# Attention and a mixture of experts in one kernel: the experts' token lists built by comparisons and matmuls of ones instead of scatters

## The chip, the core and the metric

One core of a Trainium2 chip runs the whole kernel. Its engines are TensorE (PE, whose weight loads are shown as PEld), VectorE (DVE), ScalarE (ACT), GpSimd (POOL) and SyncE (SP). The metric is the time of one execution on the device in microseconds (us). The trace counts from the start of its span.

## The reference

Attention of 8 batches, 8 heads, 576 positions and 64 dimensions, then a mixture of 8 experts over the 4608 tokens. Each token goes to the one expert with the largest logit, so the experts' work depends on lists of tokens that exist only once attention is done.

```python
q_rot, k_rot = (rotate(q), rotate(k))
scores = scale * np.matmul(q_rot, k_rot.transpose(0, 1, 3, 2))
attn = np.exp(scores - np.max(scores, axis=-1, keepdims=True))
attn = attn / (np.sum(attn, axis=-1, keepdims=True) + 1e-09)
x = np.matmul(attn, v)  # then heads are put side by side: 4608 tokens x 512
logits = x @ w_gate
e_idx = np.argmax(logits, axis=1)
gate_w = softmax(logits)[np.arange(N), e_idx]
eom = 1.0 / (1.0 + np.exp(-(x @ w_output_gate)))
for e in range(E):
    mask = e_idx == e
    h = np.maximum(x[mask] @ w1[e], 0.0)
    out[mask] = gate_w[mask, None] * eom[mask, e, None] * (h @ w2[e])
```

## The kernel before

The order of all instructions is written out by hand.

**Attention** goes over 32 pairs of heads (4 pairs to a batch). A pair has 9 steps; a step is one tile of 128 queries by 576 keys. In each step PE makes the scores in one of two PSUM buffers (`scores`, tag `sc`, L432 and L439), DVE takes their maximum (`peak`, L445), ACT makes the exponentials (`exp`, L454), and one step later DVE transposes them in blocks (`turn`, L460). All the rest is hung on steps: `EVENTS` gives, for every piece of work of a pair, its step counted from the pair's first and its place in the step. So the values of a pair (`values`, L479) are multiplied in steps 2, 4, 6 and 8 of the next pair; `back` (L494), which turns the result and multiplies it with the gates' weights, and `divide` (L502 to L511) come in its step 1; POOL rotates and splits the queries and keys of later pairs (`mult` L388, `add` L392, `keylo` and `querylo` L372) in steps 5, 7, 8, 1, 3 and 5. SP loads `raw` (queries and keys of a pair, L377) and `v` (L383).

**Placing a batch.** `place` makes a list of small functions, one to a step, that begins 20 steps after the first step of the batch's last pair. They find each token's expert (`s0` to `s7`), its output weight (`s8` to `s12`), and write the batch's tokens, 513 numbers a row, to the DRAM tensor `xd` (`s13`, two stores from SP, L590 and L591). `s14` ranks the tokens: two matmuls of ones and of a triangle (L599, L600) into `rk`, a tile taken from the same two score buffers; DVE reads it (L602, L603). `s15` to `s17` make each token's place `pi` in a long list: one stretch of 4608 places for each expert. Then five indirect DMAs from POOL (`scatter`, L616) write the token numbers, 4 bytes each, to these places, each into a DRAM list of its own, `lst0` to `lst4`; SP filled them at the start with a large number (L166). In steps of a pair, `s13` falls on a step 6, `s14` on a step 0 and the scatters on steps 6, 7, 8, 0 and 1. POOL does the elementwise steps, except in the last batch, where DVE does.

**Tables.** A table says which rows (128 tokens of one expert) a run of slots works on. Table 0 (5 slots of two rows) is made in attention, table 1 (in two parts: 9 slots of two rows, 15 of one, numbered 2 and 1) in the first expert slots. `slots` computes the row numbers on DVE, fills five tiles `tk` on POOL (L701), gathers them with five indirect DMAs from the five lists (L706), takes their minimum (four DVE instructions, L713), turns it on PE (L717) and casts it to indices. `pieces` cuts this into functions, one to a step.

**Experts.** `fetch` gathers the tokens of the first two slots (`xg`, L832), in a buffer that `xb`, the tokens of a batch, also uses. Each slot has eight steps: four of the first matrix (L888, L898), four of the second (L926). Weights come from SP (`wr`, L845), ACT and DVE or POOL split them in two (L854, L856), POOL scatters the results to the output (L938). The last batch's placing and table 1 are a queue, `left`, from which each of the eight steps of a slot takes two functions; the last batch's five scatters share entries with table 1's first five functions.

Of the kernel before, what the change touches and what calls it, by code (L numbers as in the profile page):

```python
# [10 lines left out]
F32 = mybir.dt.float32  # L11
# [25 lines left out]


# [15 lines left out]
C_E8, C_MASK, C_TOK, C_EB, C_SL, C_TRI, C_ONE = range(7)  # L54
# [16 lines left out]
def const_table(nb):  # L71
# [41 lines left out]
def body(ctx, tc, nb, offs, qk, v, rope, cst, gates, w, out):  # L113
# [39 lines left out]
    zero, big = stage[:, nst:nst + 256], stage[:, nst + 256:nst + 256 + nl // P]  # L153
    nc.vector.memset(zero, 0.0)
    nc.vector.memset(big, BIG)
# [4 lines left out]
    def consts():  # L160
        nc.vector.tensor_copy(ii[:, :, 0:P], ident.unsqueeze(1).broadcast_to((P, NP, P)))
        nc.vector.tensor_copy(trib, sc(C_TRI))
        nc.vector.tensor_copy(oneb, sc(C_ONE))
        nc.vector.memset(cnt, 0.0)
        for l in lst:
            nc.sync.dma_start(out=l.rearrange("(p n) o -> p (n o)", p=P), in_=big)  # L166

    att = Attention(tc, nb, pools, cc, ident, ii, first, trib, oneb, cnt, zero, qk, v, xd, lst)
    n0 = slot_counts(nb)[0]
    moe = Moe(tc, nb, (px, px2, small), cc, ident, cnt, w, xd, lst, out)  # L170
# [47 lines left out]
class Attention:  # L218


    def __init__(self, tc, nb, pools, cc, ident, ii, first, trib, oneb, cnt, zero, qk, v, xd, lst):
# [33 lines left out]
        for n, pr in enumerate(self.pairs):  # L255
# [259 lines left out]
def place(tc, pools, b, NT, cc, trib, oneb, cnt, xbs, xd, lst):  # L515
# [71 lines left out]
    def s13():  # L587
# [4 lines left out]
        V.tensor_scalar(new("tok", [P, NCH]), cc(C_TOK), float(b * S), None, op0=ALU.add)  # L592
# [21 lines left out]
    def scatter(c):  # L614
        m = QR if c == 4 else P
        nc.gpsimd.indirect_dma_start(  # L616
            out=lst[c][:, :], out_offset=bass.IndirectOffsetOnAxis(ap=T["pi"][:m, c:c + 1], axis=0),
            in_=T["tok"][:m, c:c + 1], in_offset=None, bounds_check=E * list_rows(NT // S) - 1, oob_is_err=False)
# [16 lines left out]
class Moe:
# [40 lines left out]
    def slots(self, n, m, ends, delta, first, step, wait):  # L676
# [28 lines left out]
        for l, tk in zip(self.lst, tks):  # L705
# [343 lines left out]
```

## Time and profile before

| | us |
|---|---|
| median of 3 runs | 1230.01 |
| lowest, highest | 1220.46, 1232.24 |
| the profiled execution | 1221.57 |
| its span | 1219.8 |
| last exponentials of attention start | 681.4 |
| first matmul of the experts starts | 717.5 |

| engine | busy us | share of the span |
|---|---|---|
| PE | 1074.2 | 88% |
| DVE | 835.0 | 68% |
| ACT | 640.2 | 52% |
| POOL | 597.9 | 49% |

The page shows one execution. A row of the timeline has start, length, engine, line, operation, what it writes and reads, how many are merged, and in brackets how long the engine stood idle before it and what ended that. A row of groups has count, busy us, mean ns of one, and idle time before with what ended it; "issue" is a wait for nothing that the profile shows. A row of waits has total us, times and the longest. Rows of stretches have, for every engine, busy us and number of instructions, then the granted share of TensorE's clock, the busy share of the DMA engines and GB/s. PEclk is that clock in 40 slices, in tenths, 9 being 90% or more.

### The profile page before, as it was taken

How to read it: one execution, taken by the hardware profiler on the slowest of the kernel's cores; microseconds unless marked ns; L12 is line 12 of the kernel's file. 1: busy time of each engine (PE TensorE's matmuls, PEld its weight loads, DVE VectorE, ACT ScalarE, POOL GpSimd, SP SyncE). 2: the span in 40 equal slices, each digit the busy share in tenths (PEclk: the TensorE clock that was granted, in tenths of full speed). 3: DMA queues.
4: the chain of work that ended last, by engine and by line, in shares of the span. 5: the costliest groups of instructions: out<-in, count | busy, mean ns of one | idle time of the engine just before them, and what ended most of it. 6: DMA issues, size and time to landing. Idle time of an engine off the chain costs nothing.

```text
span 1219.8 us, 34628 instructions
## 1 busy us (share of the span) xinstructions
PE 1074.2 (88%) x14419; PEld 919.9 (75%) x14419; DVE 835.0 (68%) x1335; ACT 640.2 (52%) x1309; POOL 597.9 (49%) x535
## 2 busy tenths in 40 slices
PE   3999985999887888989857879989999999999998
PEld 2877764777766766777646578878988989889986
DVE  6788863876765766767747347655677786786784
ACT  3566642554543544545424245433576675686573
POOL 4676765566774675575554312332154253353242
PEclk9999987988987998878868869989999999999999
DMA  6544486484675675574724647956578788797791
GB/s 206 157 143 134 120 165 80 111 164 112 153 126 86 159 113 140 131 126 110 162 36 79 213 139 210 239 191 214 185 253 301 266 298 278 272 330 263 269 338 40
DMA packets 55713, 216.87 MB, mean 178 GB/s; under 512 B 10337, under 2 KB 11260, under 8 KB 47488
## 3 DMA queue, kind: packets, MB, share of 16 engines
q1 hardware_dynamic: 46432, 194.77, 59.0%
q0 software_dynamic: 8160, 19.03, 4.6%
q8 instruction: 115, 1.88, 0.7%
q10 hardware_dynamic: 960, 0.82, 0.2%
q14 instruction: 46, 0.38, 0.1%
HBM read 195.98 MB, written 20.70 MB: 178 GB/s over the span
## 4 chain that ended last, share of the span: by engine, by line
PE 65%; DVE 12%; issue 9%; DMA 5%; ACT 4%; another core or an unknown queue 2%; POOL 2%; SPq 0%; POOLq 0%; ACTq 0%; DVEq 0%
PE py L926 15%; PE acc L479 14%; PE sc L439 14%; PE ph L898 12%; PE ph L888 4%; DVE pt L460 3%; DVE m L445 3%; PE sc L432 3%; DMA wr<-in_w 2%; PE acc L494 2%; ACT pm L454 2%; DVE wl L856 1%; PE mtp L870 1%; DMA lst<-tok,pi 1%
## 5 line engine op out<-in xcount | busy, mean ns | idle before, releaser
L454 ACT ACTIVATE pm<-sc,m 128x576 f32<-128x576 f32 x288 | 213.2, 740 | 283.1 <-DVE m L445 281.3
L445 DVE TENSOR_REDUCE m<-sc 128x1 f32<-128x576 f32 x288 | 213.7, 742 | 171.2 <-PE sc L439 156.0
L856 DVE TENSOR_TENSOR wl<-wr,wh 128x1024 fp32r<-128x1024 f32 x183 | 252.2, 1389 | 68.3 <-ACT wh L854 66.3
L479 PE MATMUL acc<-pt,v 32*64 32x160 f32 (+1 forms) x9216 | 240.1, 322 | 58.1 <-issue 33.0
L439 PE MATMUL sc<-kh,q 64*128 64x288 f32 x1024 | 239.9, 345 | 54.3 <-ACT pm L454 39.5
L479 PEld LDWEIGHTS acc<-pt,v 32*64 32x64 f32 x9216 | 184.0, 145 | 97.3 <-issue 65.0
L439 PEld LDWEIGHTS sc<-kh,q 64*128 64x128 f32 x1024 | 164.1, 207 | 103.3 <-ACT pm L454 55.8
L460 DVE STREAM_TRANSPOSE pt<-pm 128x576 f32<-128x576 f32 x288 | 220.5, 766 | 12.5 <-ACT pm L454 11.6
L854 ACT CAST wh<-wr 128x1024 fp32r<-128x1024 f32 x208 | 213.1, 1051 | 4.5 <-DMA wr<-in_w 4.4
L926 PE MATMUL py<-wh,ht 128*128 128x512 f32 x640 | 213.8, 399 | 0.0
L898 PE MATMUL ph<-xt,wh 128*128 128x256 f32 x896 | 165.9, 288 | 4.1 <-ACT xb L511 4.1
L388 POOL TENSOR_TENSOR raw<-raw,rt 128x1152 f32<-128x1152 f32 x62 | 164.0, 2646 | 9.4 <-DMA raw<-in_qk 9.3
L898 PEld LDWEIGHTS ph<-xt,wh 128*128 128x128 f32 x896 | 142.9, 195 | 6.1 <-ACT xb L511 4.6
L926 PEld LDWEIGHTS py<-wh,ht 128*128 128x128 f32 x640 | 120.2, 188 | 24.0
L898 PE MATMUL ph<-xt,wl 128*128 128x256 f32 x448 | 128.2, 286 | 0.0
L926 PE MATMUL py<-wl,ht 128*128 128x512 f32 x320 | 125.1, 391 | 0.0
L439 PE MATMUL sc<-kl,q 64*128 64x288 f32 x512 | 118.0, 315 | 0.0
L856 POOL TENSOR_TENSOR wl<-wr,wh 128x1024 fp32r<-128x1024 f32 x25 | 61.1, 2445 | 109.4 <-ACT wh L854 95.5
L439 PEld LDWEIGHTS sc<-kl,q 64*128 64x128 f32 x512 | 92.3, 210 | 0.0
L392 POOL TENSOR_TENSOR raw<-raw 128x576 f32<-128x576 f32 x62 | 87.8, 1416 | 3.2
L372 POOL TENSOR_TENSOR kl<-raw,kh 128x576 fp32r<-128x576 f32 x31 | 44.0, 1418 | 92.2 <-ACT kh L364 92.1
L898 PEld LDWEIGHTS ph<-xt,wl 128*128 128x128 f32 x448 | 87.2, 195 | 0.0
(208 smaller groups left out, 1303.0 us busy)
## 6 DMA issues: line engine op xcount, KB each, us to landing
wr<-in_w SPq DMA_DIRECT2D x208, 512.0 KB
v<-in_v SPq DMA_DIRECT2D x128, 288.0 KB
raw<-in_qk SPq DMA_DIRECT2D x31, 1152.0 KB
xd<-xb SPq DMA_DIRECT2D x8, 1026.0 KB
raw<-in_qk SPq DMA_DIRECT2D x2, 576.0 KB
xd<-xb SPq DMA_DIRECT2D x8, 128.2 KB
lst<-stage SPq DMA_DIRECT2D x5, 144.0 KB
lst<-tok,pi POOLq DMA_INDIRECT x40
```

What stands on the lines that cost most here:

```text
L388: self.eng(eng).tensor_tensor(out=rv, in0=rv, in1=self.rt[:, 2 * t:2 * t + 2, x], op=ALU.mult)
L392: self.eng(eng).tensor_tensor(out=r[:, 2 * t, x], in0=r[:, 2 * t, x], in1=r[:, 2 * t + 1, x], op=ALU.add)
L439: nc.tensor.matmul(ps[:, a, :HS], self.q[r, w, c * P:c * P + P], mov[r, a * HS:a * HS + HS], start=(n == 0), stop=(n == 2))
L445: nc.vector.tensor_reduce(self.m[i], ps[:, :, :HS], axis=AX.XY, op=ALU.max, negate=True)
L454: nc.scalar.activation(pe.rearrange("p (a b) -> p a b", a=2), self.ps[i][:, :, :HS], AF.Exp, bias=self.m[i], scale=1.0, accum_out=self.z[: ...
L460: self.nc.vector.transpose(out=self.pt[:, st[0] + 5 * st[1] if st else 4, :], in_=self.pc.pop(i))
L479: nc.tensor.matmul(self.acc[h * D:h * D + D, a, o:o + 32 * n], self.v[r, h, j, :], self.pt[r, u:u + n, 32 * j:32 * j + 32], start=(j == 0) ...
L854: self.nc.scalar.copy(wh, r)
L856: eng.tensor_tensor(out=wl, in0=r, in1=wh.bitcast(F32), op=ALU.subtract)
L888: nc.tensor.matmul(ph[:, 0, :], st[:, dc, 0:P], mv[:, dc, :], start=(n == 0), stop=(n == 11))
L898: nc.tensor.matmul(ph[:, f, :], st[:, dc, fs], mv[:, dc, :], start=(n == 0), stop=(n == 11))
L926: self.nc.tensor.matmul(py[h], st[:, f, hs], mv, start=(f == 0 and n == 0), stop=(f == 7 and n == 2))
```

## The change

The token lists live on the chip as one tile, `lists`, 128 partitions by 288 columns: column r, partition p is place 128 r + p. An empty place is 0, so token numbers are stored plus one. `s18` and `s19` split each token's place in row and column. For each of the five chunks of 128 tokens, `ones` compares: DVE makes `ro` (is this the token's row?, 288 wide, bfloat16), and V (POOL, in the last batch DVE) makes two tiles `pl` of 128 (is this its column?, times the number within the chunk plus one, and times the chunk's offset). `s20` multiplies `pl` with `ro`, ten matmuls that add up in one score buffer, and DVE adds the result to `lists`. The five scatters, the five lists, their filling and `tok` are gone.

For each table, `turned` turns `lists` on PE (three transposes into a score buffer), copies it with ACT and stores it from ACT's queue to DRAM. `slots` then gathers from this one list, and two DVE instructions turn 0 into the large number.

The steps of a batch's placing change order: `base` and the ranking come first (`s14` on a step 2 of a pair, was step 0), the output weight is spread between, `s13` with its two stores comes four steps later (step 1), `ones` are on steps 6, 7, 8, 0, 1, where the scatters were, and `s20` on a step 4. The number of steps that `done` counts by is now 39, that of the other batches, where it was 23, that of the last one; so table 0 starts 16 steps later, behind batch 5's placing instead of ahead of its ranking. Its gather is used five steps later (was ten). `fetch` stays on its step, with a buffer of its own. In `left`, the last batch has 26 functions and table 1 follows them.

```diff
     if n0:
         g = att.done(nb - 3) + 1
-        for k, f in enumerate(pieces(moe.table0(), 21)):
+        for k, f in enumerate(pieces(moe.table0(), 18)):
             att.at(g + k, 2, f)
-        att.at(att.done(nb - 2) - att.nplace + 22, 2, moe.fetch)
+        att.at(g + 18, 2, moe.fetch)
...
-        a, b, n = att.last, pieces(moe.table1(), 60), len(att.last) - NCH
-        left = a[:n] + [lambda f=f, g=g: (f(), g()) for f, g in zip(a[n:], b)] + b[NCH:]
+        left = att.last + pieces(moe.table1(), 60)
...
-    def scatter(c):
-        m = QR if c == 4 else P
-        nc.gpsimd.indirect_dma_start(
-            out=lst[c][:, :], out_offset=bass.IndirectOffsetOnAxis(ap=T["pi"][:m, c:c + 1], axis=0),
-            in_=T["tok"][:m, c:c + 1], in_offset=None, bounds_check=E * list_rows(NT // S) - 1, oob_is_err=False)
+    def s18():
+        nc.vector.tensor_scalar(new("hi", [P, NCH], I32), T["pi"], 7, None, op0=ALU.logical_shift_right)
+
+    def s19():
+        V.tensor_copy(new("hr", [P, NCH]), T["hi"])
+        V.tensor_scalar(T["hr"], T["hr"], -MID, None, op0=ALU.add)
+        lo = new("lo", [P, NCH])
+        V.tensor_scalar(lo, T["hr"], -float(P), -(P + 1) * MID, op0=ALU.mult, op1=ALU.add)
+        tt(out=lo, in0=lo, in1=T["po"], op=ALU.add)
+
+    def ones(c):
...
+        nc.vector.tensor_scalar(T["ro"][:, c, :], row, T["hr"][:, c:c + 1], None, op0=ALU.is_equal)
+        for i, x in enumerate((cc(C_P1), float(b * S + c * P))):
+            V.tensor_scalar(T["pl"][:, c, i, :], row[:, 0:P], T["lo"][:, c:c + 1], x, op0=ALU.is_equal, op1=ALU.mult)
+
+    def s20():
+        T["ls"] = small.tile(f"ls{b}").rearrange("p a b -> p (a b)")[:, 0:lists.shape[1]]
+        for c in range(NCH):
+            m = QR if c == 4 else P
+            for i in range(2):
+                nc.tensor.matmul(T["ls"], T["pl"][0:m, c, i, :], T["ro"][0:m, c, :], start=(c == 0 and i == 0),
+                                 stop=(c == 4 and i == 1))
+        nc.vector.tensor_tensor(out=lists, in0=T["ls"], in1=lists, op=ALU.add)
...
-        fs = [s0, s1, s2, no, no, s3, no, no, s4, s5, s6, s7, no, no, s8, both(s9, 1), both(s10, 2), both(s11, 3),
-              lambda: add(4), no, no, s12, s13, no, no, s14, s15, no, no, s16, s17]
+    fs = {0: s0, 1: s1, 2: s2, 5: s3, 8: s4, 10: s5, 11: s6, 12: s7, 13: add0, 14: both(lambda: add(1), 2),
+          15: both(lambda: add(3), 4), 16: s8, 17: base, 18: s14, 19: s9, 20: s15, 21: lambda: (s10(), s11()), 23: s16, 24: s12,
+          25: s17, 26: s13, 28: s18, 29: s19, 38: s20}
     for c in range(NCH):
-        fs += [lambda c=c: scatter(c)]
-    return fs
+        fs[31 + c] = lambda c=c: ones(c)
+    return [fs.get(k, lambda: None) for k in range(39)]
...
-        for l, tk in zip(self.lst, tks):
-            self.nc.gpsimd.indirect_dma_start(
-                out=tk, out_offset=None, in_=l.rearrange("(r c) o -> r (c o)", c=P),
-                in_offset=bass.IndirectOffsetOnAxis(ap=ri[0:m, :], axis=0), bounds_check=E * self.rows - 1, oob_is_err=False)
+        self.nc.gpsimd.indirect_dma_start(
+            out=tk, out_offset=None, in_=self.rowsd[:, :],
+            in_offset=bass.IndirectOffsetOnAxis(ap=ri[0:m, :], axis=0), bounds_check=E * self.rows - 1, oob_is_err=False)
         for _ in range(wait):
             yield
-        tk = tks[0]
-        for o in tks[1:]:
-            V.tensor_tensor(out=tk, in0=tk, in1=o, op=ALU.min)
+        V.tensor_scalar(g, tk, 0.5, BIG, op0=ALU.is_le, op1=ALU.mult)
+        V.scalar_tensor_tensor(out=tk, in0=tk, scalar=-1.0, in1=g, op0=ALU.add, op1=ALU.add)
...
+    def turned(self, k):
...
+        for g in range(0, N, P):
+            nc.tensor.transpose(out=tr[0:min(P, N - g), g // P, :], in_=self.lists[:, g:min(N, g + P)], identity=self.ident)
+        yield
+        n, m = N // P, N % P
+        if n:
+            nc.scalar.copy(lt[:, 0:n, :], tr[:, 0:n, :])
+            nc.scalar.dma_start(out=d[0:n * P, :].rearrange("(g p) c -> p g c", p=P), in_=lt[:, 0:n, :])
+        if m:
+            nc.scalar.copy(lt[0:m, n, :], tr[0:m, n, :])
+            nc.scalar.dma_start(out=d[n * P:N, :], in_=lt[0:m, n, :])
...
-        xg = self.px2.tile([P, NCH, XW], F32, tag="xb", name="xg")
+        xg = self.px2.tile([P, 4, XW], F32, tag="xg", name="xg", bufs=1)
```

More of the change, by code (lines that the diff above doesn't have):

```diff
@@ L36 @@
 SLOT = 256
+MID = 144.0
 NB, TAIL, PO = S // 32, 160, 192
@@ L133, in body @@
     xd = dpool.tile([NT, XW], F32, name="xd")
-    nl = E * list_rows(nb)
-    lst = [dpool.tile([nl, 1], F32, name=f"lst{c}") for c in range(NCH)]
+    nl = E * list_rows(nb) // P
+    lst = [dpool.tile([nl, P], F32, name=f"lst{c}") for c in range(2)]
     first = Pair.first(tc, pools, qk[0, 0], rope)
@@ L152, in body @@
     cnt = cpool.tile([P, E], F32, name="cnt")
-    zero, big = stage[:, nst:nst + 256], stage[:, nst + 256:nst + 256 + nl // P]
+    row = cpool.tile([P, nl], BF16, name="row")
+    lists = cpool.tile([P, nl], F32, name="lists")
+    zero = stage[:, nst:nst + 256]
     nc.vector.memset(zero, 0.0)
-    nc.vector.memset(big, BIG)
     nc.scalar.dma_start(out=ct, in_=cst[:, 0:o])
@@ L164, in consts @@
         nc.vector.memset(cnt, 0.0)
-        for l in lst:
-            nc.sync.dma_start(out=l.rearrange("(p n) o -> p (n o)", p=P), in_=big)
-    att = Attention(tc, nb, pools, cc, ident, ii, first, trib, oneb, cnt, zero, qk, v, xd, lst)
+        nc.vector.tensor_copy(row, sc(C_ROW))
+        nc.vector.memset(lists, 0.0)
+    att = Attention(tc, nb, pools, cc, ident, ii, first, trib, oneb, cnt, zero, qk, v, xd, row, lists)
     n0 = slot_counts(nb)[0]
-    moe = Moe(tc, nb, (px, px2, small), cc, ident, cnt, w, xd, lst, out)
+    moe = Moe(tc, nb, (px, px2, small), cc, ident, cnt, w, xd, lists, lst, out)
     if n0:
         g = att.done(nb - 3) + 1
-        for k, f in enumerate(pieces(moe.table0(), 21)):
+        for k, f in enumerate(pieces(moe.table0(), 18)):
             att.at(g + k, 2, f)
-        att.at(att.done(nb - 2) - att.nplace + 22, 2, moe.fetch)
+        att.at(g + 18, 2, moe.fetch)
     att.start(consts)
@@ L218, with __init__ @@
 class Attention:
-    def __init__(self, tc, nb, pools, cc, ident, ii, first, trib, oneb, cnt, zero, qk, v, xd, lst):
+    def __init__(self, tc, nb, pools, cc, ident, ii, first, trib, oneb, cnt, zero, qk, v, xd, row, lists):
         nc = tc.nc
@@ L269, in __init__ @@
             if n % NP == NP - 1:
-                fs = place(tc, (px, px2, small), b, NT, cc, trib, oneb, cnt, xbs, xd, lst)
-                self.nplace = len(fs)
+                fs = place(tc, (px, px2, small), b, NT, cc, trib, oneb, cnt, xbs, xd, row, lists)
                 if b == nb - 1:
@@ L512, in divide, with place @@
                                  scale=rz[0:QR, 8 + h:9 + h])
-def place(tc, pools, b, NT, cc, trib, oneb, cnt, xbs, xd, lst):
+def place(tc, pools, b, NT, cc, trib, oneb, cnt, xbs, xd, row, lists):
     nc = tc.nc
@@ L591, in s13, with base @@
         nc.sync.dma_start(out=xd[b * S + QM:b * S + S, :], in_=xbs[b][0:QR, 4, 0:XW])
-        V.tensor_scalar(new("tok", [P, NCH]), cc(C_TOK), float(b * S), None, op0=ALU.add)
+    def base():
         tt(out=new("base", [P, E]), in0=cnt, in1=cc(C_EB), op=ALU.add)
@@ L697, in slots @@
             V.tensor_tensor(out=row, in0=row, in1=first, op=ALU.add)
-        tks = [t([m, P], f"{n}tk{c}") for c in range(NCH)]
-        for tk in tks:
-            self.nc.gpsimd.memset(tk, BIG)
+        tk, g = t([m, P], f"{n}tk"), t([m, P], f"{n}g")
+        self.nc.gpsimd.memset(tk, 0.0)
         yield
@@ L735, in table0 @@
         V, t = self.nc.vector, self.t
+        yield from self.turned(0)
         fn, fi = self.padded("fn"), t([P, E], "fi", I32)
```

31 lines of the change are left out of this document (20 added, 11 removed).

## The prediction

> **What bounds the kernel now.** I read the page first (span, granted clock), then stretches of the attention stage (busy time, clock, DMA), then the waits and the timeline where a stretch stood out, then groups by form for durations.
>
> ```profile
> span 1219.8 us, 34628 instructions
> ...
> PEclk9999987988987998878868869989999999999999
> ```
>
> The profiled execution took 1221.57 us. TensorE has its full clock in the first 150 us and after 850 us and loses it again and again in between. In the stretches below the columns are length, busy time of PE, PEld, DVE, ACT and POOL, clock, DMA share, GB/s.
>
> ```profile
> 89.20:157.10 67.90, 62.35 (x1404) 51.85 (x1402) 57.32 (x103) 41.69 (x110) 47.09 (x46) 1.00 0.48 133
> 157.10:232.30 75.20, 58.95 (x1063) 48.15 (x1064) 43.88 (x81) 31.45 (x83) 40.80 (x38) 0.82 0.69 121
> 249.30:311.50 62.20, 57.67 (x1064) 46.85 (x1065) 43.67 (x81) 31.47 (x84) 40.78 (x38) 0.86 0.67 147
> 328.50:401.10 72.60, 59.63 (x1064) 48.61 (x1065) 43.62 (x81) 31.45 (x83) 42.00 (x39) 0.81 0.69 126
> 418.10:485.00 66.90, 54.91 (x1064) 45.39 (x1065) 43.65 (x81) 31.50 (x84) 40.99 (x38) 0.90 0.70 137
> 502.00:567.80 65.80, 61.53 (x1064) 49.69 (x1065) 43.82 (x81) 31.57 (x84) 40.91 (x38) 0.79 0.70 139
> 587.20:666.60 79.40, 58.46 (x1064) 48.43 (x1065) 50.43 (x103) 31.42 (x83) 39.69 (x50) 0.79 0.45 81
> ```
>
> The first row is four pairs of heads without a rank matmul or a scatter: 17.0 us a pair at full clock, with PE and DVE both close to full (62 and 57 of 68 us). Each further row is the three pairs in which the rank step and the scatters of one of batches 0 to 5 fall. Three clean pairs would take 51 us, so the excess is 24.2 + 11.2 + 21.6 + 15.9 + 14.8 + 28.4 = 116 us. What stands behind it decides this change.
>
> **Removed: the scatters.** 40 issues on POOL, five a batch:
>
> ```profile
> L616 POOL DMA_INDIRECT lst<-tok,pi x40 | 41.6, 1040 | 9.9 <-issue 7.0 <-POOL pi L612 2.3 <-DVE ui L759 0.3
> ```
>
> ```profile
> 178.00:187.00 9.00, 7.78 (x115) 6.08 (x115) 7.76 (x15) 5.66 (x16) 8.16 (x8) 1.00 0.90 42
> 192.00:204.00 12.00, 7.03 (x113) 5.88 (x115) 2.77 (x4) 1.66 (x4) 8.86 (x8) 0.59 0.97 52
> 212.00:221.00 9.00, 8.76 (x112) 7.25 (x112) 5.83 (x14) 4.60 (x14) 0.87 (x4) 0.66 0.58 134
> ```
>
> ```profile
> 196.97 1.38 PE L479 MATMUL acc<-pt,v 32*64 32x160 f32 x32 [7.97 <-issue]
> ```
>
> Batch 0's scatters are issued from 175 to 187 us. Then, and again from 192 to 204, the DMA engines are 90 to 97% busy and move 42 and 52 GB/s; the same kind of load (q, k and v tiles) at 212 moves 134 at 58%. From 189 to 197 PE stands 8 us inside a run of value matmuls whose data are there, for nothing that the profile shows; I read this as its instructions, which also come by DMA, being late. I take the 4-byte writes as what clogs the engines, and the second stretch, behind the last issue, as their tail. POOL is rid of (41.6 + 7.0) / 8 = 6.1 us a batch.
>
> **Moved: the rank step** (`s14`), from step 0 to step 2 of a pair.
>
> ```profile
> 158.03 0.53 PE L439 MATMUL sc<-kh,q 64*128 64x288 f32 x2 [1.62 <-ACT pm L454]
> ```
>
> ```profile
> 89.20:96.10 6.90, 5.90 (x108) 4.75 (x106) 5.47 (x13) 4.01 (x11) 3.72 (x3) 1.00 0.65 147
> 157.14:168.24 11.10, 10.21 (x114) 8.28 (x114) 6.00 (x15) 4.04 (x11) 4.24 (x4) 0.69 1.03 203
> ```
>
> ```profile
> 656.71 1.64 PE L479 MATMUL acc<-pt,v 32*64 32x160 f32 x80
> ...
> 659.87 1.37 PE L479 MATMUL acc<-pt,v 32*64 32x160 f32 x64
> ```
>
> `rk` takes one of two score buffers, so the next scores wait for the exp just before: 1.62 us, and the clock falls behind it: 0.69 over 11.1 us is 6.9 us at half, 3.4 lost. The three steps take 11.1 instead of 6.9 us, 4.2 a batch, some 25 of the 116. At step 2 the 80 value matmuls (1.64 us) run between the scores and `rk` and cover that wait; I leave 0.4 a batch, and 2 where POOL's `base`, now one step ahead, is late. The output gate's steps and the two `xd` stores move four steps back: on SP they go from ahead of a `raw` load to ahead of a `v` load that is used ten steps (19 us) later, and the store waits on POOL's copy, with only that `v` load behind it. I cost that at nothing; were the cover gone, the values would wait for what the store is late, a step or two of 1.9 us.
>
> **Added: the lists on the chip.** Durations of the nearest rows:
>
> ```profile
> L502 DVE TENSOR_TENSOR xb<-acc,rz 128x512 f32<-128x512 f32 x32 | 21.5, 670 | 10.7 <-PE acc L494 10.6
> ...
> L602 DVE TENSOR_TENSOR pr<-rk,base 128x40 f32<-128x40 f32 x8 | 1.3, 164 | 0.0
> ...
> L163 DVE CAST oneb<-stage 128x128 bf16<-128x128 f32 x1 | 0.2, 211 | 0.0
> ```
>
> ```profile
> L372 POOL TENSOR_TENSOR kl<-raw,kh 128x576 fp32r<-128x576 f32 x31 | 44.0, 1418 | 92.2 <-ACT kh L364 92.1
> ...
> L546 POOL TENSOR_SCALAR sc<-dd 128x40 f32<-128x40 f32 x7 | 2.3, 330 | 0.0
> ```
>
> ```profile
> 155.83 0.42 PE L439 MATMUL sc<-kh,q 64*128 64x288 f32 x2
> 156.19 0.20 PE L599 MATMUL rk<-ohs,oneb 128*128 128x48 bf16 x1
> ```
>
> PE: ten matmuls of 288 columns a batch. Here two of 288 columns take 0.36 us from start to the next start, 0.18 each; at the rate of the clean steps somewhat less. Ten cost 1.3 to 1.8; I take 1.5, on the path, since PE is full. Their buffer falls on step 4, behind value matmuls, as above. DVE: the sum into `lists` is 128x288 from PSUM, between 164 ns (40 wide) and 670 (512): 0.43 us, while PE does the next scores. POOL: ten comparisons of 128 wide, between 330 ns (40) and 1418 (576): 0.5 each, 5.1 a batch, with `s19` 0.9: 6.0 against 6.1 and `tok` removed. POOL comes out even.
>
> The dear part is `ro`, five DVE comparisons a batch, 128x288, by themselves 0.2 (the cast of 128) to 0.4 us. They fall on steps 6, 7, 8, 0, 1, where POOL has its longest multiplications. What DVE meets there:
>
> ```profile
> L713 DVE TENSOR_TENSOR 0tk<-0tk,0tk 10x128 f32<-10x128 f32 x4 | 4.5, 1122 | 0.1
> ...
> L739 DVE TENSOR_SCALAR fi<-fi 128x8 int32<-128x8 int32 x1 | 2.5, 2535 | 0.0
> ...
> L713 DVE TENSOR_TENSOR 2tk<-2tk,2tk 18x128 f32<-18x128 f32 x4 | 1.1, 280 | 6.3 <-DMA 2tk<-lst,2ri 6.3
> ```
>
> ```profile
> 643.67 2.72 POOL L388 TENSOR_TENSOR raw<-raw,rt 128x1152 f32<-128x1152 f32 x1
> 643.68 4.59 DVE L713 TENSOR_TENSOR 0tk<-0tk,0tk 10x128 f32<-10x128 f32 x4
> ```
>
> The minimum of `2tk`, in the expert stage, takes 280 ns; that of `0tk`, beside POOL's multiplication, 1122; an 8-wide shift took 2.5 us. So each `ro` may stand up to 2.5 us; I take 0.7, about the mean rest of a POOL instruction (2.7, 1.4 or 0.5 us long), so 5 x (0.3 + 0.7) = 5 us a batch on an engine that is 85% full. I put 3 on the path, and one fall of the clock behind it: 3.4 lost, as behind `rk` now. A batch then costs 0.4 + 1.5 + 3 + 3.4 = 8.3 us, at least 2 (all hidden, clock kept) and at most 22 (2.5 each, two falls); six batches 50.
>
> [...]
>
> **Table 0.** Five gathers and four minima become one gather and two DVE steps, all of it 16 steps later; three transposes, two copies and two stores on ACT's queue come ahead.
>
> ```profile
> PE sc L439 <- ACT pm L454: 17.8, 5, 11.9
> ...
> ACT q L364 <- POOL raw L392: 13.6, 1, 13.6
> POOL 0tk L706 <- DMA lst<-tok,pi: 11.8, 2, 6.0
> ```
>
> These are the waits of 587 to 667 us: POOL's gathers waited 11.8 us for scatters, the next `q` was late by 13.6, PE stood 11.9. In the new order the stores have ten steps to land, the gather five. What remains is a buffer taken twice without cover (2 x 1.6), some DVE instructions held by POOL and a clock loss: 9 us (4 to 12). Attention in all: 50 + 9 - 116 = -57.
>
> At the start five fills of the lists leave SP's queue and one cast and one memset come to DVE, some 0.5 us between the constants: nothing.
>
> **The turn to the experts.**
>
> ```profile
> 686.50:705.40 18.90, 16.23 (x289) 9.76 (x289) 0.20 (x1) 0.01 (x1) 9.55 (x11) 0.66 0.62 241
> ```
>
> ```profile
> L832 POOL DMA_INDIRECT xg<-xd,0idx x4 | 4.2, 1038 | 10.1 <-DMA xd<-xb 9.2 <-issue 0.9
> ```
>
> The last 288 value matmuls take 18.9 us here; four runs of 80 and 64 would take 6.0 (rows above). During them POOL issues four gathers, late by 9.2 for a buffer that `xg` no longer shares, and five scatters. I give back half of 12.9 and charge 1.5 for the last lists: -5 (-12 to +3).
>
> **Experts.**
>
> ```profile
> POOL out L938 <- DVE xt L873: 18.1, 1, 18.1
> ...
> PE 2tr L717 <- DVE 2tk L713: 8.4, 1, 8.4
> ...
> PE 1tr L717 <- DVE 1tk L713: 2.6, 1, 2.6
> ```
>
> ```profile
> 790.20:851.30 61.10, 50.19 (x308) 45.82 (x309) 33.32 (x66) 23.51 (x31) 19.25 (x23) 0.92 0.64 208
> ```
>
> POOL's stores stand 18 us behind the last batch's scatters, so table 1's gathers come late and PE stands 8.4 us, later some 2.6 for `1tr`, and at clock 0.92 another 4.9 of 61 are lost: 16 in all. The two copies and stores of table 1 go to ACT, 24 of 61 us busy there, at nothing. New: `s20` stands in the same step as the last `ones`, which DVE reaches behind a cast's rest and `xt`; PE waits some 3, 1.5 for the matmuls, 3.4 for the clock: 8. Net -8 (-14 to +2).
>
> **The sum.** 1221.6 - 57 - 5 - 8 = 1151.6, say 1150 us. The profiled execution lies 8 us under the median of the runs (1230.01); I add nothing for that, since the spread may be the scatters' own. Faster by 6%. About 1% is what a measurement of this kernel tells from no change.
>
> **Rivals.** *Clean*: the list work hides wholly: 2 x 6 + 4 in attention (-100), -11 and -14: 1096. For it: POOL comes out even and steps 6 and 8 have slack; against: DVE's 85%. *Not the scatters*: the slow loads have another cause, as the stretch at 192, after the last issue, allows. Then only `rk` (25) and table 0's waits (16) go, 75 stays and 59 comes: +18, with the turn's -5: 1235. *Slower*: DVE stands behind POOL. 30 `ro` of 2.5 us, with two clock losses a batch, cost 22 x 6 = 132, table 0 12: 144 against 116, so +28, the turn -5: 1245. It decides from 18 us a batch on, a stand of about 2 us each; against it, the 2.7 us multiplications are rarely just begun when a `ro` comes.
>
> **How the numbers follow.** Forecast 0.60 (its own range 1115 to 1185), clean 0.22, not the scatters 0.07, slower 0.06, and 0.05 for half an effect near 1200. So faster by over 1% 0.87, within 1% 0.05, slower 0.08. The range 1095 to 1200 leaves out the last two and the cleanest.
>
> **What would show it.** Right: no stretch with 90% DMA share under 60 GB/s; PE's waits for issue gone; the `rk` wait under 0.5; groups of three pairs near 59 us; `ro` at about 1 us mean, with the clock falling once behind it; `2tr` without a wait. Wrong: slow stretches that stay without scatters; `ro` near 0.3 (clean) or over 2 us (slower); PE waiting at `s20` in attention.

## The result, and the profile after

| | before | changed |
|---|---|---|
| median of the runs beside each other | 1231.12 us (4 runs) | 1174.61 us (4 runs) |
| lowest, highest | 1220.46, 1234.74 | 1168.54, 1181.74 |
| the profiled execution | 1221.57 | 1177.33 |
| its span | 1219.8 | 1175.6 |
| last exponentials start | 681.4 | 646.0 |
| first matmul of the experts starts | 717.5 | 673.3 |

The changed kernel takes 0.955 of the time before (95% interval 0.948 to 0.963): 4.5% faster, where 6% was forecast. A second set of runs of the same kernel, among the experiments, gave 0.952 (0.947 to 0.957). All ratios here are of fast runs, those within 1.5% of the fastest of their kernel, which leaves out two of ten runs of `e2_scat4` and two of six of `e5_xd5`. The page of the changed kernel:

```profile
span 1175.6 us, 34808 instructions
...
PEclk9999998898999988989887798999999999999998
```

Stretches of the changed kernel; columns are length, busy us and number of instructions of PE, PEld, DVE, ACT and POOL, granted clock, DMA share, GB/s. The first row is three pairs with nothing but the rank step in them, then the three pairs of each of batches 0 to 5 as in the prediction's table, then the last pair:

```profile
108.50:159.20 50.70, 46.54 (x1054) 38.80 (x1053) 43.56 (x80) 30.90 (x81) 35.22 (x39) 1.00 0.49 137
160.20:218.80 58.60, 53.13 (x1068) 43.94 (x1068) 47.08 (x84) 31.28 (x83) 43.31 (x49) 0.91 0.59 147
239.00:301.10 62.10, 53.87 (x1068) 44.25 (x1067) 48.75 (x84) 31.25 (x82) 42.45 (x49) 0.92 0.55 139
318.80:376.60 57.80, 50.90 (x1068) 42.01 (x1068) 46.49 (x84) 31.34 (x83) 43.56 (x49) 0.97 0.58 150
394.20:454.30 60.10, 51.94 (x1068) 42.37 (x1068) 46.43 (x84) 31.38 (x82) 43.52 (x49) 0.94 0.54 144
474.50:537.30 62.80, 54.52 (x1069) 44.99 (x1068) 47.35 (x84) 31.43 (x83) 42.76 (x49) 0.89 0.50 138
554.90:621.50 66.60, 56.11 (x1073) 45.74 (x1073) 49.10 (x105) 32.00 (x85) 40.71 (x51) 0.90 0.39 97
621.50:646.00 24.50, 21.71 (x337) 17.56 (x339) 13.50 (x30) 7.74 (x21) 5.05 (x8) 0.65 0.56 168
```

The six groups take 368.0 us; before they took 422.1. Each still runs at a clock of 0.89 to 0.97, not 1.00. No stretch of 9 or 12 us between 90 and 650 us has a DMA share of 0.90 or more and less than 60 GB/s. The stretches that were clogged before, 42 and 52 GB/s at a share of 0.90 and 0.97, now read:

```profile
178.00:187.00 9.00, 8.36 (x88) 6.64 (x78) 8.48 (x18) 4.33 (x14) 8.72 (x9) 0.59 0.73 191
192.00:204.00 12.00, 11.99 (x195) 9.97 (x190) 9.64 (x17) 7.15 (x19) 10.21 (x8) 1.00 0.57 167
```

PE's waits for nothing that the profile shows, from 89 to 560 us, in the kernel before (total us, times, longest):

```profile
PE acc L479 <- issue: 29.9, 19, 8.0
PE sc L439 <- issue: 3.4, 1, 3.4
```

and in the changed one:

```profile
PE acc L481 <- issue: 12.2, 8, 4.2
PE sc L441 <- issue: 2.8, 2, 2.4
```

They fell from 33.3 to 15.0 us and are not gone; a second profiled execution (`e9_after`) has 12.7. They fit the prediction's reading that PE's instructions come late: in that stretch all five of over 1 us in the changed kernel end 1.3 to 2.1 us behind the landing of a 16 KB packet of the instruction queue `q8`, and each of these packets started 8 to 13 us after the one before it (4 to 10 us in clean attention). In the kernel before, five of seven end 1.1 to 1.4 us behind one. What makes these packets start late is not shown.

The turn to the experts, the second expert slot, the two slots in which `2tr` and `1tr` stood, and the time behind the last matmul, in the changed kernel:

```profile
646.00:673.30 27.30, 14.39 (x347) 10.89 (x331) 10.26 (x25) 7.64 (x18) 8.79 (x15) 0.81 0.61 163
698.30:730.70 32.40, 28.68 (x169) 24.56 (x168) 19.23 (x48) 12.59 (x18) 4.51 (x4) 0.89 0.83 278
753.90:801.00 47.10, 47.10 (x308) 42.56 (x309) 32.12 (x60) 23.61 (x31) 10.32 (x10) 1.00 0.70 223
1163.80:1175.60 11.80, 0.00 (x0) 0.00 (x0) 0.00 (x0) 0.69 (x1) 0.97 (x1) 0.69 0.05 19
```

and before:

```profile
681.40:717.50 36.10, 23.16 (x339) 14.81 (x326) 8.77 (x20) 7.56 (x18) 9.55 (x11) 0.70 0.57 186
743.50:766.90 23.40, 23.40 (x157) 21.35 (x155) 17.59 (x52) 11.93 (x16) 12.74 (x13) 1.00 1.09 284
...
1214.10:1219.80 5.70, 0.00 (x0) 0.00 (x0) 0.00 (x0) 0.69 (x1) 0.97 (x1) 0.86 0.11 37
```

The turn is 8.8 us shorter, the second slot 9.0 longer (the last batch's lists are in it), and the end, in which PE is done and ACT and POOL work for 0.7 and 1.0 us, is 6.1 us longer, which was not forecast. The two slots in which `2tr` and `1tr` stood took 61.1 us before (a row of the prediction) and take 47.1 now; neither waits.

### The profile page after: what moved, and what is told of

Same layout as the page of the kernel before. It is cut to its first block, busy times and chain, and to the rows that moved or that the text cites. A ratio compares the mean times of both kernels' runs of the same rounds, so it can differ in the third digit from the quotient of the medians.

```text
span 1175.6 us, 34808 instructions
## 1 busy us (share of the span) xinstructions
PE 1056.1 (90%) x14505; PEld 908.4 (77%) x14505; DVE 860.3 (73%) x1399; ACT 641.0 (55%) x1313; POOL 598.2 (51%) x562
## 4 chain that ended last, share of the span: by engine, by line
PE 69%; DVE 14%; issue 8%; ACT 4%; DMA 3%; SPq 0%; POOL 0%; ACTq 0%; POOLq 0%; DVEq 0%
PE py L972 16%; PE acc L481 15%; PE sc L441 14%; PE ph L944 13%; DVE pt L462 4%; PE ph L934 4%; DVE m L447 4%; PE sc L434 3%; ACT pm L456 2%; PE mtp L916 1%; DVE wl L902 1%; DVE xb L504 1%; ACT xb L513 1%; PE acc L496 1%; DMA v<-in_v 1%
## 5 line engine op out<-in xcount | busy, mean ns | idle before, releaser
L902 DVE TENSOR_TENSOR wl<-wr,wh 128x1024 fp32r<-128x1024 f32 x183 | 252.6, 1391 | 65.2 <-ACT wh L900 62.8
L481 PE MATMUL acc<-pt,v 32*64 32x160 f32 (+1 forms) x9216 | 219.7, 315 | 57.9 <-ACT xb L513 34.3
L441 PE MATMUL sc<-kh,q 64*128 64x288 f32 x1024 | 235.8, 338 | 36.7 <-ACT pm L456 21.2
L481 PEld LDWEIGHTS acc<-pt,v 32*64 32x64 f32 x9216 | 174.9, 141 | 87.3 <-ACT xb L513 44.2
L441 PEld LDWEIGHTS sc<-kh,q 64*128 64x128 f32 x1024 | 161.1, 201 | 79.2 <-ACT pm L456 39.0
L390 POOL TENSOR_TENSOR raw<-raw,rt 128x1152 f32<-128x1152 f32 x62 | 164.2, 2648 | 9.6 <-DMA raw<-in_qk 9.3
L944 PE MATMUL ph<-xt,wh 128*128 128x256 f32 x896 | 161.0, 282 | 0.5 <-ACT xb L513 0.5
L944 PEld LDWEIGHTS ph<-xt,wh 128*128 128x128 f32 x896 | 139.0, 190 | 2.4 <-ACT xb L513 1.0
L441 PE MATMUL sc<-kl,q 64*128 64x288 f32 x512 | 115.6, 309 | 0.0
L441 PEld LDWEIGHTS sc<-kl,q 64*128 64x128 f32 x512 | 89.2, 203 | 2.5 <-issue 2.5
L394 POOL TENSOR_TENSOR raw<-raw 128x576 f32<-128x576 f32 x62 | 87.7, 1414 | 2.7
```

Of the source, the lines that this page charges most:

```text
L390: self.eng(eng).tensor_tensor(out=rv, in0=rv, in1=self.rt[:, 2 * t:2 * t + 2, x], op=ALU.mult)
L394: self.eng(eng).tensor_tensor(out=r[:, 2 * t, x], in0=r[:, 2 * t, x], in1=r[:, 2 * t + 1, x], op=ALU.add)
L441: nc.tensor.matmul(ps[:, a, :HS], self.q[r, w, c * P:c * P + P], mov[r, a * HS:a * HS + HS], start=(n == 0), stop=(n == 2))
L481: nc.tensor.matmul(self.acc[h * D:h * D + D, a, o:o + 32 * n], self.v[r, h, j, :], self.pt[r, u:u + n, 32 * j:32 * j + 32], start=(j == 0) ...
L902: eng.tensor_tensor(out=wl, in0=r, in1=wh.bitcast(F32), op=ALU.subtract)
L944: nc.tensor.matmul(ph[:, f, :], st[:, dc, fs], mv[:, dc, :], start=(n == 0), stop=(n == 11))
```

## The experiments

Each set of runs has its own runs of the kernel before beside it, with medians of 1233.0, 1240.0 and 1230.3 us; so kernels are compared by their ratio to those. 1% is 12 us. Times of parts are from one profiled execution of each run. "The 24 pairs" are the fifth to the 28th pair, in which batches 0 to 4 are placed: 498.0 us before, 463.3 and (second set) 466.8 us in the changed kernel; 24 clean pairs of 17.0 us would be 408.

### The scatters: put back, and put back with longer rows

`e2_scat4` puts the five scatters beside the lists (steps 26 to 30 of the placing); `e3_scat512` differs from it in the row that each token writes, 512 bytes instead of 4, so that the rows lie 128 times as far apart, and in the tile it comes from:

```diff
+    dummy = [dpool.tile([nl * P, 1], F32, name=f"dum{c}") for c in range(NCH)]
...
+        nc.gpsimd.indirect_dma_start(
+            out=dummy[c][:, :], out_offset=bass.IndirectOffsetOnAxis(ap=T["pi"][:m, c:c + 1], axis=0),
+            in_=T["po"][:m, c:c + 1], in_offset=None, bounds_check=E * list_rows(NT // S) - 1, oob_is_err=False)
```

and from there to the other:

```diff
-    dummy = [dpool.tile([nl * P, 1], F32, name=f"dum{c}") for c in range(NCH)]
+    dummy = [dpool.tile([nl * P, P], F32, name=f"dum{c}") for c in range(NCH)]
...
-            in_=T["po"][:m, c:c + 1], in_offset=None, bounds_check=E * list_rows(NT // S) - 1, oob_is_err=False)
+            in_=ident[:m, :], in_offset=None, bounds_check=E * list_rows(NT // S) - 1, oob_is_err=False)
```

> The changed kernel with the five scatters of a batch put back beside the lists, for batches 0 to 6: each issue writes one 4-byte value per token into lists of their own that nothing reads. My theory (4-byte writes clog the DMA engines, and PE's instructions come late): stretches with 90% DMA share under 60 GB/s return behind each batch's scatters, PE stands 3 to 10 us for issue in most of them, and the time goes up by 45 to 75 us, to 1220 to 1250. Rival (not the scatters): POOL has 1 us more per issue, 35 us at 51% busy, mostly hidden: 1175 to 1185, no slow stretches.

> As the run with 4-byte scatters beside the lists, but each token writes a row of 512 bytes, into lists 128 times as large that nothing reads. If it is the shortness of the writes that clogs the engines, the slow stretches are gone although there are as many writes and 128 times the bytes (0.3 MB an issue batch, a fifth of what one pair loads): 1175 to 1195. If it is their number, or the gathering of one address per token, they stay and the time is that of the 4-byte run, 1220 to 1250.

Measured: 1.0005 (0.9967 to 1.0042) with 4-byte rows, so all that the change gains is lost again, 55 to 60 us against the 0.952 to 0.955 of the changed kernel. With 512-byte rows 0.951 (0.944 to 0.958): nothing. Waits of PE for issue from 89 to 560 us with 4 bytes:

```profile
PE acc L483 <- issue: 30.3, 10, 7.2
...
PE sc L443 <- issue: 10.9, 4, 4.0
```

and with 512:

```profile
PE acc L483 <- issue: 11.2, 4, 4.1
```

Stretches behind scatters of 4 bytes, with the DMA share (summed packet times, which can pass 1) over full and PE idle for 29 to 48% of the time:

```profile
166.00:175.00 9.00, 5.23 (x117) 4.13 (x117) 2.84 (x5) 2.22 (x5) 8.12 (x10) 1.00 1.03 43
504.00:513.00 9.00, 6.38 (x112) 5.05 (x118) 3.53 (x7) 2.22 (x5) 8.14 (x9) 0.80 1.08 53
429.00:441.00 12.00, 6.19 (x124) 5.18 (x112) 7.22 (x10) 2.92 (x8) 11.28 (x11) 0.64 1.08 123
```

and one with 512:

```profile
178.00:187.00 9.00, 7.18 (x67) 5.57 (x56) 9.00 (x11) 3.33 (x11) 8.89 (x9) 0.69 0.76 201
```

The expectation of under 60 GB/s holds behind three of six batches' scatters (the first two rows are of this kind); behind the others, as in the third row, loads of `v` and stores of `xd` fall into the same stretch. The packets show it better: of the 9216-byte packets between 140 and 660 us, 461 of 5864 took over 1.5 us before (up to 8.0), 288 of 5940 with 4-byte scatters, 4 of 6008 with 512-byte ones, 3 of 6068 in the changed kernel. So the rival that it was not the scatters is out, and it is not their number: as many writes of 512 bytes cost nothing. Since the longer rows also lie further apart, these runs do not tell whether it is the shortness of a write that counts or that many of them fall close together. Why such writes hold the others up, no run here shows.

### The rank step alone

`e1_rank` is the kernel before with the whole placing of a batch, scatters too, two steps later; `e7_rank0` is the changed kernel with the rank step (and `base`) two steps earlier, on step 0 of its pair:

```diff
-PLACE, PM = 20, 3
+PLACE, PM = 22, 3
```

```diff
-          15: both(lambda: add(3), 4), 16: s8, 17: base, 18: s14, 19: s9, 20: s15, 21: lambda: (s10(), s11()), 23: s16, 24: s12,
+          15: lambda: (add(3), add(4), base()), 16: lambda: (s8(), s14()), 19: s9, 20: s15, 21: lambda: (s10(), s11()), 23: s16, 24: s12,
```

> The kernel before with one change: the whole placement of a batch, the rank step and the five scatters with it, two steps later, so that the rank step falls on step 2 of a pair. My theory (the rank step costs 4.2 us a batch and the scatters by themselves most of the rest): some 20 to 30 us go, so about 1200; the stretches with 90% DMA share under 60 GB/s stay, and so do PE's long waits for issue; the 24 pairs from the fifth to the 28th, 498.0 us before and 463.3 in the changed kernel, take about 475. Rival (the scatters are harmless and the rank step's wait and the clock behind it are the gain): about 1180, the 24 pairs near 463.

> The changed kernel with the rank step back on step 0 of a pair, where the kernel before has it. My prediction's price (1.62 us wait and the clock behind it, 4.2 a batch less 0.4): about 23 to 27 us more, near 1200, with the wait of 1.6 us for the exp in each of the six pairs. Rival (the clock falls in these pairs by another wait anyway, so that only the wait itself counts): 5 to 12 us more, 1180 to 1187. In the run of the kernel before with the placement two steps later the pairs of the rank step were no shorter, which speaks for the rival.

Measured: 0.985 (0.979 to 0.991) for `e1_rank`, 19 us, near the 20 to 30 expected; but its 24 pairs take 500.7 us against 498.0, so within these pairs nothing was won. Their waits for issue are longer than before:

```profile
PE acc L479 <- issue: 36.0, 12, 5.7
PE sc L439 <- issue: 19.2, 5, 10.4
```

What its profiled execution won lies behind the 28th pair: 7 us up to the last exponentials and 13 in the turn (23.5 us for 36.1). So this run does not give the price of the rank step: the scatters moved with it, and PE's waits for issue grew from 33.3 to 55.2 us. That the clock falls in these pairs either way, as long as scatters stand there, would fit and is not shown.

`e7_rank0`: 0.973 (0.969 to 0.977), 21 to 25 us above the changed kernel; its 24 pairs take 501.4 us in the profiled execution. But it does not test the 1.62 us by itself. PE's waits:

```profile
PE rk L604 <- POOL ohs L580: 18.9, 6, 3.2
```

With the new order of steps, POOL's sums `ohs`, one step ahead, are late by up to 3.2 us each time. So the time is near the 1200 expected, but for another reason. What it shows is the price of a wait of that length in a pair that otherwise runs mostly at full clock: the six pairs with the rank step take 137.6 us where the changed kernel's take 110.8 and 109.4, about 4.6 more for each wait of 3.2, at a clock of 0.79 to 0.92. The 24 pairs as a whole take 35 to 38 us more; the rest lies in the other pairs.

### The lists left out

`e6_nolist` leaves `ones` and `s20` out for batches 0 to 5, so that the experts work on other rows; only its attention is read, in its one execution.

```diff
+    if b < NT // S - 2:
+        s20 = lambda: None
...
-        fs[31 + c] = lambda c=c: ones(c)
+        fs[31 + c] = lambda c=c: ones(c) if b == NT // S - 2 else None
...
```

> The changed kernel without the comparisons and the matmuls of ones of batches 0 to 5 (the steps up to hi and lo stay); their tokens are in no list, so the experts' part works on other rows and only the attention part is read; a memset of the gather's buffer is added behind attention. The 24 pairs from the fifth to the 28th take 463.3 us with the lists and would take 407 clean. My prediction's price for the lists (1.5 + 3 + 3.4 a batch): five batches of about 8, so some 423 to 430 here. If the lists hide nearly wholly and the rest has another cause, 455 or more.

The 24 pairs, without the lists:

```profile
89.60:524.30 434.70, 391.97 (x8461) 325.42 (x8460) 349.70 (x636) 250.70 (x660) 288.63 (x295) 0.97 0.55 146
```

and with them:

```profile
91.60:554.90 463.30, 412.73 (x8512) 341.03 (x8511) 369.44 (x666) 250.86 (x661) 326.64 (x345) 0.94 0.52 137
```

The lists cost 28.6 us, 5.7 a batch (6.4 against the second profiled run), less than the 7.9 of the prediction. And 434.7 is not 408: 26.7 us, 5.3 a batch, are lost with neither scatters nor lists; 3.6 of them are the six pairs of the rank step, 17.6 us instead of 17.0. Nearly all the rest, 22.4 us, is in ten of the pairs: the five in which `xd` is stored and the five right behind them. PE's waits for issue in these 24 pairs,

```profile
PE acc L481 <- issue: 9.9, 7, 2.4
PE acc L496 <- issue: 1.2, 1, 1.2
```

are 11.1 us, and a clock of 0.97 over 434.7 us is about 13 us more: together about what is left.

### What `ro` waits for

The group of the 30 `ro` in attention has a mean of 731 ns, where an undisturbed one takes 245 to 256:

```profile
L635 DVE TENSOR_SCALAR ro<-row,hr 128x288 bf16<-128x288 bf16 x30 | 21.9, 731 | 0.0
```

In the timeline (start, length), two of them, one beside POOL's multiplication and one not, then two beside POOL's `pl`:

```profile
259.59 2.63 POOL L390 TENSOR_TENSOR raw<-raw,rt 128x1152 f32<-128x1152 f32 x1
259.62 2.69 DVE L635 TENSOR_SCALAR ro<-row,hr 128x288 bf16<-128x288 bf16 x1
263.60 0.24 DVE L635 TENSOR_SCALAR ro<-row,hr 128x288 bf16<-128x288 bf16 x1
...
182.38 0.80 POOL L637 TENSOR_SCALAR pl<-row,lo,ct 128x128 bf16<-128x128 bf16 x1
182.84 0.42 DVE L635 TENSOR_SCALAR ro<-row,hr 128x288 bf16<-128x288 bf16 x1
...
498.44 0.72 POOL L637 TENSOR_SCALAR pl<-row,lo 128x128 bf16<-128x128 bf16 x1
498.77 0.25 DVE L635 TENSOR_SCALAR ro<-row,hr 128x288 bf16<-128x288 bf16 x1
```

259.59 + 2.63 = 262.22, and `ro` ends at 262.31. All ten long ones (0.85 to 2.69 us) end 0.09 to 0.10 us behind a multiplication or sum of POOL's (L390, L394), up to which they stood. Seven more, of 0.30 to 0.42 us, end 0.09 us behind a `pl` of POOL's, which has one input of 128 columns and takes 0.72 or 0.80 us; the row at 182.84 is one. But five `ro` begin and end within a `pl` in 0.25 to 0.26 us, as the row at 498.77 does. So a short instruction of POOL's can hold `ro` up too, for a short time (seven of 30) and not always. `e4_stride` has the 30 `ro` read `row` with a stride of two elements; the author's estimate was that the long stands go with it and 3 to 10 us of the whole, or, if they stay, 1175 us or a little above:

```diff
+    row2 = cpool.tile([P, nl, 2], BF16, name="row2")[:, :, 0]
...
-        nc.vector.tensor_scalar(T["ro"][:, c, :], row, T["hr"][:, c:c + 1], None, op0=ALU.is_equal)
+        nc.vector.tensor_scalar(T["ro"][:, c, :], row2, T["hr"][:, c:c + 1], None, op0=ALU.is_equal)
```

> [...] In the changed kernel they take 245 to 288 ns by themselves, but 10 of the 30 in attention 0.8 to 2.7 us, beside a multiplication on POOL. [...]

```profile
L637 DVE TENSOR_SCALAR ro<-row,hr 128x288 bf16<-128x288 bf16 x30 | 24.0, 800 | 0.0
```

```profile
255.40 2.63 POOL L392 TENSOR_TENSOR raw<-raw,rt 128x1152 f32<-128x1152 f32 x1
255.43 2.81 DVE L637 TENSOR_SCALAR ro<-row,hr 128x288 bf16<-128x288 bf16 x1
259.52 0.32 DVE L637 TENSOR_SCALAR ro<-row,hr 128x288 bf16<-128x288 bf16 x1
```

The stands stayed, and 0.948 (0.946 to 0.951) is no different from the changed kernel. The shortest `ro` grew from 0.245 to 0.320 us, so the stride adds 75 ns to an `ro` that does not stand. The one of 2.81 us ends 0.21 us behind POOL's instruction (258.24 and 258.03), where the one of 2.69 us ended 0.09 behind its own. That the stands would go with the stride was the author's estimate, and the run is against it; what of POOL's instruction holds `ro` up is not shown.

`e10_roact` takes DVE out of it:

```diff
-        nc.vector.tensor_scalar(T["ro"][:, c, :], row, T["hr"][:, c:c + 1], None, op0=ALU.is_equal)
+        nc.scalar.activation(T["sq"][:, c, :], row, AF.Square, bias=T["nh"][:, c:c + 1], scale=1.0)
+        nc.scalar.activation(T["ro"][:, c, :], T["sq"][:, c, :], AF.Relu, bias=one1, scale=-1.0)
```

> The changed kernel with `ro` made by ACT (the square of row minus hr, then the positive part of one minus it: ten instructions of 288 wide a batch) in place of five comparisons on DVE; one more POOL instruction of 128x5 a batch. Ten of the 30 `ro` stand 0.8 to 2.7 us on DVE, and each ends as POOL's multiplication or sum ends. If these stands reach the path: no such stand is left and 5 to 15 us go, 1160 to 1170 on the scale of 1175; the 24 pairs from the fifth to the 28th fall from 463 towards 450. If DVE's slack hides them, or ACT's ten instructions delay the exps as much: within 4 us of the changed kernel.

Measured: 0.9485 (0.943 to 0.954) beside 0.952 (0.947 to 0.957) for the unaltered kernel in the same set, 1166.8 and 1171.4 us: at most a little, and not told apart. The 24 pairs take 456.2 us (463.3 and 466.8). So 7 to 11 us are won there between single executions, net of what ACT's ten instructions of 0.53 us a batch cost.

### The remaining waits for issue: the store of `xd`

In the changed kernel four of PE's five waits for issue of over 1 us are in a pair with `xd` stores. `e5_xd5` spreads the store:

```diff
-        nc.sync.dma_start(out=xd[b * S:b * S + QM, :].rearrange("(c p) d -> p c d", p=P), in_=xbs[b][:, 0:4, 0:XW])
-        nc.sync.dma_start(out=xd[b * S + QM:b * S + S, :], in_=xbs[b][0:QR, 4, 0:XW])
+        keep(0)
...
+    def keep(c):
+        m = QR if c == 4 else P
+        nc.sync.dma_start(out=xd[b * S + c * P:b * S + c * P + m, :], in_=xbs[b][0:m, c, 0:XW])
...
+            fs[26 + c] = kept(fs.get(26 + c, lambda: None), c)
```

> The changed kernel, with a batch's 1154 KB for `xd`, stored in one step by two issues, stored in five pieces over five steps. In the changed kernel PE still stands 1.9 to 4.2 us for issue once a batch, 8 to 16 us behind that store, with the 16 KB instruction fetches 10 to 13 us apart instead of 6. Theory (the burst of the store with the loads of `v` and `raw` behind it is what delays the fetches): those stands fall under 1 us, the clock falls less often, and 10 to 20 us go: 1155 to 1165. Rival (the loads alone do it, or the fetch is late for another reason): they stay, 1172 to 1180.

Measured: 0.9375 (0.932 to 0.943), 18 to 22 us under the changed kernel, as much as expected (all six runs have a median of 0.942). The reason given for it fell all the same. `e11_roact_xd5` has this store and `ro` on ACT:

> Both the store of `xd` in five pieces and `ro` on ACT. If the burst of the store and the stands of `ro` are two separate losses, their gains add: 15 to 25 us under the changed kernel, 0.925 to 0.94 of the kernel before, and the best of all. If the clock falls are shared (one lost fall is won only once), the time is that of the better of the two alone.

Measured: 0.938 (0.932 to 0.943), 1154.9 us beside 1171.4 for the changed kernel in the same set. It is level with `e5_xd5`. Whether the gains add, the runs do not tell: that of `ro` on ACT alone, 4.6 us between medians, is within the noise. PE's waits for issue, with the store in five pieces:

```profile
PE acc L481 <- issue: 9.1, 6, 3.0
PE sc L441 <- issue: 2.8, 2, 2.3
```

and with `ro` on ACT as well:

```profile
PE acc L483 <- issue: 14.2, 7, 4.0
PE sc L443 <- issue: 3.6, 1, 3.6
```

11.9 and 17.8 us beside 15.0 and 12.7 in two executions of the changed kernel: a burst of stores is not what makes the instructions late. What grew shorter are the two pairs of each batch with the stores and the lists, 12 pairs in all: 250.8 (`e5_xd5`) and 254.9 us (`e11_roact_xd5`), beside 263.4 and 272.2 in two executions of the changed kernel. Over the 24 pairs of `e5_xd5` all of PE's waits sum to 39.7 us, beside 50.0 and 49.1; the clock is 0.94, beside 0.94 and 0.93. The largest part is the wait for the divided values (`xb`), 22.8 us beside 26.6 twice; no single wait makes up the gain, and why they shrink stays open.

`e8_all` puts more together: the stride, the five pieces, `og` a step later, and the second-last batch's stores and lists among the experts' first steps.

> The changed kernel with four things at once: the row of `ro` with a stride of two, the store of `xd` in five pieces, the reduction `og` in step 1 instead of step 0 of a pair (in step 0 it stands ahead of the division that the next values wait for, 0.15 us), and the stores, comparisons and matmuls of the second-last batch moved from the turn to the experts into the first expert's steps, two a step. [...] If the bursts are not the cause and the turn's 5.9 us stand for issue comes from the weights' loads, 1165 to 1172.

Measured: 0.940 (0.937 to 0.943), no better than the five pieces alone. The turn fell from 27.3 to 22.8 us, towards the author's estimate of 20, and the experts from their first matmul to the middle of the second slot grew from 39.3 to 47.3: the lists were moved, not hidden.

### The longer end

> The changed kernel once more, unaltered, as the measure for the runs beside it: 0.945 to 0.960 of the kernel before.

Its ratio is the 0.952 of the first section, and its end is 11.8 us long too. POOL's queue at the end, kernel before (length in ns, least, median and largest of three):

```profile
L1033 POOLq DRAIN  x3: 46/107/2399, 1216.5 to 1219.5; - x3
```

changed kernel, and the one with 35 scatters beside the lists:

```profile
L1079 POOLq DRAIN  x3: 46/107/6852, 1167.9 to 1175.3; - x3
```

```profile
L1088 POOLq DRAIN  x3: 46/107/9711, 1223.4 to 1233.7; - x3
```

POOL issues 135, 83 and 118 indirect DMAs in them. `e12_more` adds 52 to the changed kernel, to have 135:

```diff
+            if j in (1, 3):
+                self.nc.gpsimd.indirect_dma_start(
+                    out=self.dum[:, :], out_offset=bass.IndirectOffsetOnAxis(ap=self.idx[0][:, 0:1], axis=0),
+                    in_=self.ident[:, :], in_offset=None, bounds_check=self.NT - 1, oob_is_err=False)
```

> The changed kernel with two more indirect stores a slot in the experts' part, 52 in all (128 rows of 512 bytes into a buffer that nothing reads), so that POOL issues 135 in all, as in the kernel before, in place of 83. Behind the last matmul the kernel before takes 5.7 us to its end, the changed one 11.8 and the one with 35 scatters beside the lists 15.0: POOL's last drain is 2.4, 6.9 and 9.7 us long, with 135, 83 and 118 issues. If the drain goes by the number of issues since they were last taken back, and that happens between 118 and 135: the tail falls to about 5.7 us. If it only grows with the number: about 17. If it is the long scatters' own or has nothing to do with the number: 11.8.

```profile
L1084 POOLq DRAIN  x3: 46/107/2279, 1184.7 to 1187.5; - x3
```

The drain is short again at 135 issues: 2.3 us with 52 stores of 512-byte rows among them, where the kernel before has 2.4 us with 40 scatters of 4 bytes. So in these four executions it went with their number, not with the length of the writes: 6.9 us at 83, 9.7 at 118, 2.4 and 2.3 at 135. What makes it short again between 118 and 135 is not shown. As a whole the kernel is slower, 0.967 (0.961 to 0.972), since the added stores cost 4.5 to 5.4 us in each of four slots, and its end is 8.5 us long where 5.7 was expected.

## Why the prediction was right, and where it was off

The direction, the mechanism and the range held; the size was 70 us and became 44, counted in spans (1219.8 to 1175.6). Between medians it is 56.5 us: the profiled execution before was a quick one of its kind, and the changed kernel's was not. By its own terms, in spans:

**The six groups of attention: -57 forecast, -54.1 measured** (422.1 to 368.0; 375.9, so -46.2, in the second profiled execution). That the sum is right is luck, because two parts are wrong and cancel. Without lists (`e6_nolist`) the six groups take 342.6 us, 36.6 above the 306 of clean pairs, where the prediction leaves 11.4 (0.4 a batch and table 0's 9). The lists add 25.4 to that, where it has 47.4 (7.9 a batch). In detail:

- *Scatters.* The changed kernel with its lists and 4-byte scatters is back at the time before, so beside the lists they cost 55 to 60 us; in the profiled execution 29 of these are in the 24 pairs and 15 in the turn. The prediction gave them all of the excess of 116 that was not the rank step, 91, of which 16 as table 0's waits. It took three clean pairs, 51 us, for what is left without scatters. That step failed: without scatters and lists 5.3 us a batch remain.
- *Lists.* 8.3 us a batch forecast, 7.9 of it for the lists; 5.7 measured. `ro` has a mean of 0.73 us where 1.0 was taken, and the long stands are at POOL's multiplications and sums, as argued.
- *Rank step.* Where the wait for the exp was, there is none left: no row of PE's waits in the changed kernel names `rk`. What its 25 us were worth by themselves stays open: `e1_rank` won nothing in those pairs, but it moved the scatters too, and `e7_rank0` has another wait.
- *The store of `xd`.* Its move was put at nothing, and what the move costs was not tried. But the store is not free where it stands now: in five pieces it makes the kernel 18 to 22 us faster (`e5_xd5`).

**What lies beside the groups: nothing forecast, +18 measured.** The rank step now falls in the pair ahead of each group, because the new list reaches it seven steps earlier. Six such pairs take 110.8 us where they took 104.4. The last pair takes 24.5 instead of 14.7: the ranking of batch 6, the turn of table 0 (PE waits 1.4 us for `0idx`) and four gathers are in it, and its clock is 0.65, so 8.6 of its 24.5 us are lost to it. In the second profiled run it took 18.6, and the three pairs before it 69.5. The second pair took 1.9 us more. That makes 6.4 + 9.8 + 1.9; in the second profiled run it is 11, so how the loss divides between the groups and the pairs beside them varies from one execution to the next. Table 0's 9 us (4 to 12) were too few in the first execution.

**The turn: -5 forecast, -8.8 measured**, within its -12 to +3. PE still stands 5.9 us there for issue, and twice for the second-last batch's `s20`.

**Experts: -8 forecast, -6.1 measured** up to the last matmul, both halves as argued: 14.0 us won where `2tr` and `1tr` stood (16 forecast), and 9.0 lost in the slot of the last `s20` (8 forecast). There PE waits for `pl`, not for `ro`:

```profile
PE ls L645 <- DVE pl L637: 3.6, 2, 1.9
```

**The end: +6.1**, not in the prediction. It did not ask what POOL's queue does behind the last store.

-54.1 + 18.1 - 8.8 - 6.1 + 6.1 = -44.8, and the first exponentials start 0.4 us later.

Of what was to be seen: no clogged stretch (right), `2tr` without a wait (right), groups near 59 us (57.8 to 62.8, and 66.6 with table 0), PE's waits for issue gone (wrong, 15.0 of 33.3 us stay). The rival that it was not the scatters is refuted by their return, the clean one by the lists' 5.7 us a batch; the slower one would have needed `ro` of 2 us each.

## What to carry to other kernels

35 scatters of 4-byte writes cost this kernel 55 to 60 us: where an index list has to go through DRAM, try rows of 512 bytes, or build the list on the chip; here writing the one cost nothing (0.951 beside 0.952 to 0.955), though nothing read it, and the other cost 5.7 us a batch. Do not take the time of a clean stretch for what a busy one becomes when one cause is gone: leave the cause out in an experiment, or keep a share for the causes behind it: here 5.3 us a batch remained with neither scatters nor lists. And when steps are moved, list every pair they now fall in, not only the ones that had them before.

## What the runs showed of the hardware

- 35 scatters of up to 128 rows cost 55 to 60 us with 4-byte rows (1.0005 of the kernel before, where the changed kernel has 0.952 to 0.955) and nothing with 512-byte rows (0.951), with 128 times the bytes, 128 times as far apart.
- In the changed kernel ten of the 30 `ro`, a DVE comparison with one SBUF input, took 0.85 to 2.69 us and ended 0.09 to 0.10 us behind a POOL instruction with two inputs (the longest beside one of 2.63 us). Beside POOL's comparison with one input, seven of the 30 took 0.30 to 0.42 us and ended 0.09 us behind it, and five ran through within it in 0.25 to 0.26.
- In the stretch 160 to 219 us of the changed kernel the longest that PE stood was 2.3 us, and half clock began 0.6 us behind that wait and lasted 10.2 us (0.91 over the stretch). At 222.9 and 458.4 us it began 0.5 to 0.6 us behind waits of 1.1 us and lasted 6.8 us.
- The last drain of POOL's queue took 6.9 us after 83 indirect DMAs, 9.7 after 118, and 2.4 and 2.3 after 135.
